# Recurrent attention and a two-layer feed-forward on one core: beta's halves exchanged by ScalarE, u's sign moved into a diagonal, GpSimd's low weight parts in one piece, and a new order of all steps

## The chip, the core and the metric

The kernel runs on one core of one Trainium2 chip. The metric is the device time of one execution in microseconds. The core's engines run side by side, each with its own queue in program order, and wait for each other by semaphores: TensorE (PE in the profile, PEld for its weight loads), VectorE (DVE), ScalarE (ACT), GpSimd (POOL) and SyncE (SP, which here only issues transfers).

## The reference

A recurrence over 768 time steps in 4 batches and 8 heads of width 48, and then a feed-forward over its 3072 rows of 384 numbers:

```python
for t in range(S):
    cur = np.einsum('bhd,bhe->bhde', u[None] * kt, vt)
    y[:, :, t] = np.einsum('bhd,bhde->bhe', rt, state + cur)
    state = wt[:, :, :, None] * state + np.einsum('bhd,bhe->bhde', kt, vt)
...
h = np.maximum(x @ w_in, 0.0)      # w_in is 384 x 2048
return (h * h @ w_out)             # w_out is 2048 x 384
```

The term with u gives each time step a number per head, the sum over d of r·u·k, which multiplies v of the same step. It is called beta below.

## The kernel before

The 768 steps are cut into 6 chunks of 128, and a unit is one chunk of one batch, 24 units in all (chunk c, batch b). Inside a unit the decays are multiplied up by scans on DVE (L538), r and k are scaled by them, TensorE makes a matrix of scores of 128 by 128 steps in quarters, and a mask keeps the part below the diagonal. The diagonal of that matrix is beta. ACT writes it as eight pieces of 64 columns, a constant diagonal times a column of beta each (L634, L749), before DVE lays the masked scores over it (L713, L763).

For chunk 0 beta comes from TensorE (L579). For the later chunks POOL multiplies r by k (L588) and by u (L590), and DVE sums over d (L593); `un` holds minus u in all rows, made so by one POOL instruction (L394), since k and the scores carry a minus sign. The sum has time steps in its 128 rows and the 8 heads in its columns, and the layout of the scores wants the lower 64 rows of one half of the heads exchanged with the upper 64 rows of the other half. Three DVE instructions of 64 rows by 4 columns do it, as the maximum of a number with itself (L596, L597, L598), the second and third each reading or overwriting what the one before has set free.

The feed-forward works in full precision by splitting each factor into a high part and a low part: three products instead of one. Both weight matrices come in 8 groups. For each group and matrix ("wi", "wo") ACT widens the raw bits (L430), DVE puts the number together in three instructions (L434, L438, L443), ACT rounds it to the high part (L450), and POOL subtracts to get the low part (L452), 768 columns in two instructions of 384. The plan marks DVE steps with `port=True` where it counts them as in POOL's way.

For one step f of the feed-forward (16 a chunk; the first six of chunk 0 and all of chunk 1 are cut into two halves of two batches) TensorE makes `hp` with nine products (L866), ACT takes the positive part (L871), ACT (chunk 0, L873) or DVE (later chunks, L875) squares it, ACT casts it to the high part of g (L877), DVE subtracts for the low part of g (L878), and TensorE adds three products a batch to `ob` (L884). PSUM holds two `hp`, two `a` and four `ob`.

The program is a list of steps, each with an engine, a cost and the keys that it reads and writes (`P.add`). The order in which they are issued is a table of step numbers (`ORDER`), found by a search outside the kernel; `PLACES` says which buffer a slot takes, and `FILLS` in front of which steps TensorE runs idle transposes (L352), and how many: `146: (3, 'hp', 0)` is three of them before step 146. Each engine's queue is this one order with the other engines' steps left out, SP's transfers too.

Of the kernel before, what the change touches and what calls it, by code (L numbers as in the profile page):

```python
# [9 lines left out]
F32 = mybir.dt.float32  # L10
# [4 lines left out]
AF = mybir.ActivationFunctionType  # L15
# [81 lines left out]
class Names:  # L97
# [133 lines left out]
def kernel(  # L231
# [50 lines left out]
    Q = C // 2  # L282
# [742 lines left out]
```

## Time and profile before

| | |
|---|---|
| median of 3 runs | 516.04 us (515.96 to 516.71) |
| the profiled execution | 517.37 us |
| its span, first to last instruction | 515.3 us, granted TensorE clock 0.997 |
| PE busy | 501.4 us, 97% of the span |
| PEld busy | 455.2 us, 88% |
| DVE busy | 359.6 us, 70% |
| ACT busy | 318.1 us, 62% |
| POOL busy | 107.0 us, 21% |
| idle transposes (L352) | 16 at the start, then 48 |

The shares are means over the whole span. The engines' load differs much between the first quarter and the rest, so they are read by stretches. A matrix product's end is modelled, and products overlap, so PE can be busy by this account and still lose a little.

### The profile page before, as it was taken

How to read it: one execution, taken by the hardware profiler on the slowest of the kernel's cores; microseconds unless marked ns; L12 is line 12 of the kernel's file. 1: busy time of each engine (PE TensorE's matmuls, PEld its weight loads, DVE VectorE, ACT ScalarE, POOL GpSimd, SP SyncE). 2: the span in 40 equal slices, each digit the busy share in tenths (PEclk: the TensorE clock that was granted, in tenths of full speed). 3: DMA queues.
4: the chain of work that ended last, by engine and by line, in shares of the span. 5: the costliest groups of instructions: out<-in, count | busy, mean ns of one | idle time of the engine just before them, and what ended most of it. 6: DMA issues, size and time to landing. Idle time of an engine off the chain costs nothing.

```text
span 515.3 us, 13724 instructions
## 1 busy us (share of the span) xinstructions
PE 501.4 (97%) x5416; PEld 455.2 (88%) x5416; DVE 359.6 (70%) x799; ACT 318.1 (62%) x870; POOL 107.0 (21%) x157
## 2 busy tenths in 40 slices
PE   8999999899999999999999999999999999999995
PEld 7888888789999999989998898898899888998894
DVE  6998899989778988868768477777466464324231
ACT  4999898889766767576564655663634353423232
POOL 2235951864040221303004002103000000000000
PEclk9999999999999999999999999999999999999998
DMA  8999899716837477483652662661161010200001
GB/s 161 222 225 251 184 207 194 138 21 93 153 56 123 90 107 141 80 137 55 103 115 54 118 99 33 103 123 37 39 115 32 1 21 12 67 1 1 1 0 66
DMA packets 188311, 48.73 MB, mean 95 GB/s; under 512 B 178001, under 2 KB 183122, under 8 KB 188242
## 3 DMA queue, kind: packets, MB, share of 16 engines
q1 hardware_dynamic: 187664, 47.01, 48.1%
q8 instruction: 44, 0.72, 0.6%
q10 hardware_dynamic: 578, 0.79, 0.4%
q14 instruction: 25, 0.20, 0.1%
HBM read 31.66 MB, written 4.72 MB: 71 GB/s over the span
## 4 chain that ended last, share of the span: by engine, by line
PE 81%; SPq 6%; DMA 4%; issue 3%; DVE 2%; ACT 2%; POOL 1%; POOLq 0%; DVEq 0%
PE ob L884 36%; PE hp L866 35%; PE ob L672 2%; SPq L507 2%; PE ob L691 2%; PE a L681 2%; SPq L474 2%; SPq L417 2%; PE a L654 1%; PE hp L639 1%; DMA st<-in_r_dram 1%; DMA ri<-in_moe_w_in_dram 1%; DMA v<-in_v_dram 1%; POOL wi L452 1%; ACT m L634 1%
## 5 line engine op out<-in xcount | busy, mean ns | idle before, releaser
L884 PE MATMUL ob<-wo,g 128*128 128x384 f32 x1152 | 226.7, 340 | 0.4 <-POOL wo L452 0.2
L866 PE MATMUL hp<-x,wi 128*128 128x512 f32 (+1 forms) x1062 | 222.2, 355 | 2.1 <-DVE g L878 1.4
L884 PEld LDWEIGHTS ob<-wo,g 128*128 128x128 f32 x1152 | 199.5, 188 | 8.7 <-DVE g L878 0.8
L866 PEld LDWEIGHTS hp<-x,wi 128*128 128x128 f32 x1062 | 174.9, 188 | 27.9 <-DVE g L878 2.4
L871 ACT ACTIVATE t<-hp 128x512 f32<-128x512 f32 (+1 forms) x118 | 61.0, 517 | 76.4 <-PE hp L866 48.6
L875 DVE SCALAR_TENSOR_TENSOR hp<-hp,t 128x512 f32<-128x512 f32 (+1 forms) x96 | 58.2, 606 | 69.6 <-ACT t L871 68.7
L878 DVE TENSOR_TENSOR g<-hp,g 128x512 fp32r<-128x512 f32 (+1 forms) x118 | 69.2, 587 | 38.5 <-ACT g L877 37.7
L877 ACT CAST g<-hp 128x512 fp32r<-128x512 f32 (+1 forms) x118 | 59.6, 506 | 46.1 <-DVE hp L875 45.2
L662 POOL MEMSET S<- 1x1 f32 x20 | 1.8, 88 | 242.4 <-PE ob L672 242.3
L634 ACT ACTIVATE m<-diag,beta 128x64 f32<-128x64 f32 x160 | 40.3, 340 | 1.2 <-DVE beta L597 1.1
L615 ACT ACTIVATE x<-ob 112x128 fp32r<-112x128 f32 x80 | 19.6, 278 | 22.6 <-PE ob L691 16.1
L618 DVE SCALAR_TENSOR_TENSOR x<-ob,x 112x128 fp32r<-112x128 f32 x80 | 20.8, 282 | 18.1 <-ACT x L615 15.7
L828 ACT COPY ob<-zero 112x128 f32<-112x128 f32 x80 | 20.6, 271 | 17.4 <-DVE x L618 10.9
L538 DVE TENSOR_TENSOR_SCAN pt<-pt,zero 112x128 f32<-112x128 f32 x64 | 25.8, 435 | 1.9 <-DMA v<-in_v_dram 1.1
L588 POOL TENSOR_TENSOR st<-st 128x384 f32<-128x384 f32 x20 | 22.0, 1107 | 22.4 <-DVE st L483 20.7
L452 POOL TENSOR_TENSOR wi<-q,wi 128x384 fp32r<-128x384 f32 x16 | 22.5, 1429 | 19.5 <-ACT wi L450 19.5
L452 POOL TENSOR_TENSOR wo<-q,wo 128x384 fp32r<-128x384 f32 x16 | 18.3, 1164 | 26.6 <-ACT wo L450 26.5
L590 POOL TENSOR_TENSOR st<-st,un 128x384 f32<-128x384 f32 x20 | 21.6, 1085 | 0.9
L483 DVE STREAM_TRANSPOSE st<-st 128x1152 f32<-128x1152 f32 x16 | 21.5, 1359 | 0.4 <-ACT st L609 0.4
L713 DVE COPY_PREDICATED m<-caus,a 128x256 f32<-128x256 uint8 x40 | 17.2, 441 | 3.2 <-PE a L654 3.1
L562 DVE TENSOR_TENSOR pt<-pt,m 112x512 f32<-112x512 f32 x24 | 18.0, 751 | 0.4
L545 ACT ACTIVATE m<-pt 112x512 f32<-112x512 f32 x24 | 15.2, 634 | 4.6 <-DVE pt L538 4.0
(126 smaller groups left out, 535.6 us busy)
## 6 DMA issues: line engine op xcount, KB each, us to landing
pt<-st SPq DMA_DIRECT2D x96, 96.0 KB, 3.0
ro<-in_moe_w_out_dram SPq DMA_DIRECT2D x8, 768.0 KB, 6.7
v<-in_v_dram SPq DMA_DIRECT2D x96, 48.0 KB, 2.9
out_dram<-q SPq DMA_DIRECT2D x20, 192.0 KB, 2.1
ri<-in_moe_w_in_dram SPq DMA_DIRECT2D x32, 96.0 KB, 5.2
ri<-in_moe_w_in_dram SPq DMA_DIRECT2D x8, 384.0 KB, 7.7
st<-in_k_dram SPq DMA_DIRECT2D x8, 384.0 KB, 5.2
st<-in_r_dram SPq DMA_DIRECT2D x8, 384.0 KB, 5.8
```

What stands on the lines that cost most here:

```text
L452: P.add("pool", 1.0, rank(8 * k + 5), lambda q=q, tt=tt, z=z: G.tensor_tensor(out=tt[:, 1, z * 384:z * 384 + 384], in0=q.tile[:, z * 384:z ...
L483: V.transpose(out=zt[:, i].rearrange("a t p q i -> a t (p q) i"), in_=sv[:, :, i].rearrange("s t p q x -> s t (p q) x"))
L538: lambda p=p: V.tensor_tensor_scan(out=pt[:, 0, p], data0=src(0)[:, p], data1=zero.broadcast_to([HP, C]), initial=1.0, op0=ALU.mult, op1=A ...
L588: P.add("pool", 0.97, rank("rk"), lambda: G.tensor_tensor(out=rk(), in0=rk(), in1=vals(2), op=ALU.mult), r=[(st, ui, 2)], w=[(st, ui, 1)])
L590: P.add("pool", 0.97, rank("ru"), lambda: G.tensor_tensor(out=rk(), in0=rk(), in1=un.rearrange("s (h d) -> s h d", d=D), op=ALU.mult), r=[ ...
L634: A.activation(M.tile[:, o:o + Q], diag2, AF.Copy, scale=beta.tile[:, i:i + 1])
L866: T.matmul(hp.tile[:, 0:n], wi[f][:, wl, kt], xT[:, kt, xl, xs], start=(m == 0), stop=(m == 3 * KT - 1))
L871: P.add("act", 0.49 if full else 0.28, rank("g1"), lambda: A.activation(t(), h(), AF.Relu), r=[hp], w=[(g, 1)])
L875: P.add("dve", 0.605 if full else 0.337, rank("g2"), lambda: V.scalar_tensor_tensor(out=h(), in0=h(), scalar=0.0, in1=t(), op0=ALU.max, op ...
L877: P.add("act", 0.48 if full else 0.26, rank("g3"), lambda: A.copy(out=hi(), in_=h()), r=[hp], w=[(g, 0)])
L878: P.add("dve", 0.605 if full else 0.335, rank("g4"), lambda: V.tensor_tensor(out=lo(), in0=h(), in1=hi().bitcast(F32), op=ALU.subtract), r ...
L884: T.matmul(obs[b][:, 0:DM], g.tile[0][:, gl, o:o + C], wo[f][:, wl], start=(f == 0 and m == 0), stop=(f == NF - 1 and m == 2))
```

## The change

Five things change.

1. Beta's exchange: three ACT copies take the place of the three DVE instructions. It is a step of ACT now, with 0.45 as cost in the plan.
2. u's sign: the POOL instruction on `un` goes. A second constant diagonal, `diag3`, the negative of the first, is made at the start by two scaled ACT copies, and the diagonals of chunks 1 to 5 are made from it.
3. POOL's low weight parts: one instruction of 768 columns for each group and matrix, 16 in place of 32. The keys ("rest", 0) and ("rest", 1) become one.
4. There are 17 steps fewer, so all numbers in the tables change.
5. The order, the places and the fills are those of a new search. The sum of the fills is 59 in place of 48.

```diff
 FILLS = {
-    15: (3, 'ob', 0), 56: (5, 'ob', 1), 58: (5, 'ob', 1), 37: (2, 'ob', 1), 42: (3, 'ob', 1), 83: (4, 'ob', 3), 146: (3, 'hp', 0), 125: (11, 'ob', 0),
-    128: (2, 'ob', 0), 130: (5, 'ob', 0), 166: (2, 'side', 0), 169: (3, 'side', 0),
+    14: (3, 'ob', 0), 30: (8, 'ob', 1), 55: (7, 'ob', 1), 71: (1, 'ob', 0), 48: (8, 'ob', 1), 82: (3, 'ob', 0), 89: (12, 'ob', 0), 145: (2, 'ob', 0),
+    463: (2, 'ob', 0), 159: (5, 'ob', 0), 127: (2, 'side', 0), 168: (6, 'side', 0),
 }
...
+    diag3 = at.tile([128, Q], F32, name="diag3")
...
         A.copy(out=diag2[hs], in_=ident[hs, hs])
+        A.activation(diag3[hs], ident[hs, hs], AF.Copy, scale=-1.0)
...
-        P.add("pool", 1.1, "un", lambda: G.tensor_scalar(out=un, in0=un, scalar1=-1.0, scalar2=None, op0=ALU.mult), w=["un"])
...
-            for z in range(2):
-                P.add("pool", 1.0, rank(8 * k + 5), lambda q=q, tt=tt, z=z: G.tensor_tensor(out=tt[:, 1, z * 384:z * 384 + 384], in0=q.tile[:, z * 384:z * 384 + 384], in1=tt[:, 0, z * 384:z * 384 + 384].bitcast(F32), op=ALU.subtract),
-                      r=[q, lead], w=[(nm, g, "rest", z)])
+            P.add("pool", 1.9, rank(8 * k + 5), lambda q=q, tt=tt: G.tensor_tensor(out=tt[:, 1], in0=q.tile, in1=tt[:, 0].bitcast(F32), op=ALU.subtract),
+                  r=[q, lead], w=[(nm, g, "rest")])
...
             def halves():
-                V.tensor_tensor(out=beta.tile[s1, H:], in0=beta.tile[s2, h1], in1=beta.tile[s2, h1], op=ALU.max)
-                V.tensor_tensor(out=beta.tile[s2, h1], in0=beta.tile[s1, h2], in1=beta.tile[s1, h2], op=ALU.max)
-                V.tensor_tensor(out=beta.tile[s1, h2], in0=beta.tile[s1, H:], in1=beta.tile[s1, H:], op=ALU.max)
-            P.add("dve", 0.46, rank("bh"), halves, w=[beta], port=True)
+                A.copy(out=beta.tile[s1, H:], in_=beta.tile[s2, h1])
+                A.copy(out=beta.tile[s2, h1], in_=beta.tile[s1, h2])
+                A.copy(out=beta.tile[s1, h2], in_=beta.tile[s1, H:])
+            P.add("act", 0.45, rank("bh"), halves, w=[beta])
...
-                            A.activation(M.tile[:, o:o + Q], diag2, AF.Copy, scale=beta.tile[:, i:i + 1])
+                            A.activation(M.tile[:, o:o + Q], diag2 if summed else diag3, AF.Copy, scale=beta.tile[:, i:i + 1])
```

What the new order makes of it is shown at three places. Line numbers of the changed kernel are smaller by one from L452 on (L878 becomes L877).

DVE near the end of chunk 0's feed-forward, before the change: the second reduction for beta, a low part of g, the first unit's exchange, and the next low part of g.

```order
L593 TENSOR_REDUCE beta_177<-st_143 128x8
L443 SCALAR_TENSOR_TENSOR q_156<-ro_70,q_156 128x768
L878 TENSOR_TENSOR g_95<-hp_151,g_95 128x256
L562 TENSOR_TENSOR pt_135<-pt_135,m_167 112x512
L596 TENSOR_TENSOR beta_176<-beta_176 64x4
L597 TENSOR_TENSOR beta_176<-beta_176 64x4
L598 TENSOR_TENSOR beta_176<-beta_176 64x4
L818 TENSOR_TENSOR S_140<-a_153,Ec_172 112x96
L878 TENSOR_TENSOR g_97<-hp_152,g_97 128x512
```

The same place on DVE after the change:

```order
L877 TENSOR_TENSOR g_99<-hp_152,g_99 128x256
L592 TENSOR_REDUCE beta_177<-st_144 128x8
L592 TENSOR_REDUCE beta_178<-st_144 128x8
L877 TENSOR_TENSOR g_95<-hp_153,g_95 128x512
L434 TENSOR_SCALAR q_156<-q_156 128x768
L438 SCALAR_TENSOR_TENSOR q_156<-ri_76,q_156 128x768
L555 TENSOR_TENSOR pt_136<-pt_136 112x4x127
L443 SCALAR_TENSOR_TENSOR q_156<-ri_76,q_156 128x768
L877 TENSOR_TENSOR g_97<-hp_152,g_97 128x512
```

Both reductions stand together ahead of a low part of g, the exchange is gone, and a weight's joining stands between two low parts of g.

ACT at the same place after the change: the positive part (L870), the square (L872) and the cast to the high part (L876) of a feed-forward step, and what stands between them and the next step's.

```order
L870 ACTIVATE t_98<-hp_152 128x512
L872 ACTIVATE hp_152<-t_98 128x512
L595 COPY beta_178<-beta_178 64x4
L596 COPY beta_178<-beta_178 64x4
L597 COPY beta_178<-beta_178 64x4
L876 CAST g_97<-hp_152 128x512
L430 ACTIVATE q_157<-ro_78 128x768
L827 COPY ob_151<-zero 112x128
L450 CAST wi_77<-q_156 128x768
L870 ACTIVATE t_100<-hp_153 128x512
L872 ACTIVATE hp_153<-t_100 128x512
L876 CAST g_99<-hp_153 128x512
```

The exchange of the first unit that gets one stands between the square and the cast of one step.

POOL's first weight parts, before the change:

```order
L394 TENSOR_SCALAR un<-un 128x384
L452 TENSOR_TENSOR wi_57<-q_155,wi_57 128x384 x2
L452 TENSOR_TENSOR wo_59<-q_156,wo_59 128x384 x2
L452 TENSOR_TENSOR wi_61<-q_155,wi_61 128x384 x2
L452 TENSOR_TENSOR wi_65<-q_156,wi_65 128x384 x2
```

And after it:

```order
L451 TENSOR_TENSOR wi_57<-q_156,wi_57 128x768
L451 TENSOR_TENSOR wo_59<-q_157,wo_59 128x768
L451 TENSOR_TENSOR wi_61<-q_156,wi_61 128x768
L451 TENSOR_TENSOR wi_65<-q_157,wi_65 128x768
L451 TENSOR_TENSOR wo_63<-q_156,wo_63 128x768
```

The negation is gone and each pair is one instruction; the sequence of these parts is the same.

## Rows read from the trace of the kernel before

**Rows 1.** Busy time by stretches: from:to, length, then each engine's busy us (instructions)

```profile
12.00:45.00 33.00, 30.77 (x485) 27.14 (x484) 31.44 (x66) 31.17 (x93) 12.42 (x9) 1.00 0.99 226
45.00:130.00 85.00, 81.44 (x833) 72.81 (x837) 78.84 (x144) 76.98 (x190) 48.11 (x43) 1.00 0.74 148
130.00:430.00 300.00, 299.73 (x3579) 273.98 (x3569) 214.73 (x512) 176.87 (x523) 43.37 (x83) 1.00 0.47 83
```

**Rows 2.** PE's waits in the whole span: us in total, times, longest

```profile
PE a L352 <- POOL ident masks.py:199: 1.6, 1, 1.6
PE hp L866 <- DVE g L878: 1.4, 2, 0.8
PE ob L691 <- issue: 1.3, 2, 1.2
...
PE hp L866 <- POOL wi L452: 0.6, 1, 0.6
PE hp L639 <- DVE g L878: 0.4, 1, 0.4
...
PE hp L521 <- DVE g L878: 0.3, 1, 0.3
PE ob L884 <- POOL wo L452: 0.2, 1, 0.2
```

**Rows 3.** Timeline of PE at 41 and 77 us: start, us, what, idle before

```profile
41.50 2.18 PE L866 MATMUL hp<-x,wi 128*128 128x256 f32 x16 [0.55 <-POOL wi L452]
...
77.07 1.67 PE L866 MATMUL hp<-x,wi 128*128 128x512 f32 x6 [0.79 <-DVE g L878]
```

**Rows 4.** Timeline of DVE from 72.5 us: start, us, what

```profile
72.55 0.41 DVE L878 TENSOR_TENSOR g<-hp,g 128x256 fp32r<-128x256 f32 x1
...
74.06 1.02 DVE L596 TENSOR_TENSOR beta<-beta 64x4 f32<-64x4 f32 x1
75.12 0.95 DVE L597 TENSOR_TENSOR beta<-beta 64x4 f32<-64x4 f32 x1
76.10 0.15 DVE L598 TENSOR_TENSOR beta<-beta 64x4 f32<-64x4 f32 x1
...
76.35 0.67 DVE L878 TENSOR_TENSOR g<-hp,g 128x512 fp32r<-128x512 f32 x1
```

**Rows 5.** Timeline of POOL, two stretches: start, us for both halves, idle before

```profile
37.41 4.03 POOL L452 TENSOR_TENSOR wi<-q,wi 128x384 fp32r<-128x384 f32 x2 [4.08 <-ACT wi L450]
...
70.79 2.71 POOL L452 TENSOR_TENSOR wi<-q,wi 128x384 fp32r<-128x384 f32 x2 [3.49 <-ACT wi L450]
74.05 2.00 POOL L452 TENSOR_TENSOR wo<-q,wo 128x384 fp32r<-128x384 f32 x2 [0.55 <-ACT wo L450]
```

**Rows 6.** Groups of instructions from 0 to 130 us: count, busy us, mean ns

```profile
L597 DVE TENSOR_TENSOR beta<-beta 64x4 f32<-64x4 f32 x6 | 3.0, 494 | 0.2
L596 DVE TENSOR_TENSOR beta<-beta 64x4 f32<-64x4 f32 x6 | 2.4, 402 | 0.1
```

**Rows 7.** Timeline of DVE from 123 us: start, us, what

```profile
123.18 1.39 DVE L597 TENSOR_TENSOR beta<-beta 64x4 f32<-64x4 f32 x1
...
127.60 0.42 DVE L878 TENSOR_TENSOR g<-hp,g 128x256 fp32r<-128x256 f32 x1
```

**Rows 8.** Timeline of ACT at 127 us: start, us, what

```profile
127.21 0.36 ACT L877 CAST g<-hp 128x256 fp32r<-128x256 f32 x1
```

**Rows 9.** Groups of instructions in the whole span: count, busy us, mean ns

```profile
L561 ACT COPY Ec<-pt 112x4 f32<-112x4 f32 x20 | 3.9, 195 | 1.5 <-DVE pt L538 1.5
L452 POOL TENSOR_TENSOR wi<-q,wi 128x384 fp32r<-128x384 f32 x16 | 22.5, 1429 | 19.5 <-ACT wi L450 19.5
```

**Rows 10.** Timeline of ACT at the start: start, us, what, idle before

```profile
2.10 0.50 ACT L365 COPY diag<-ident 64x64 f32<-64x64 f32 x2
...
6.17 0.69 ACT L548 ACTIVATE pt<-ob,one_sided 112x512 f32<-112x512 f32 x1 [3.57 <-PE ob L521]
```

**Rows 11.** Timeline of PE at 27 us: start, us, what

```profile
27.12 1.42 PE L352 MATMUL ob<-ident 128*128 128x128 f32 x11
```

More of the change, by code (lines that the diff above doesn't have):

```diff
@@ L859, in ffn @@
         hp, g = Slot("hp"), Slot("g")
-        wkeys = lambda nm: [(nm, f // 2, "lead"), (nm, f // 2, "rest", 0), (nm, f // 2, "rest", 1)]
+        wkeys = lambda nm: [(nm, f // 2, "lead"), (nm, f // 2, "rest")]
         def first():
```

203 rows, old and new, of tables (ORDER, PLACES) are left out of this document.

## The prediction, made before the run

> **What bounds the kernel now.** I read the busy time by stretches first [rows 1]. From 130 to 430 us TensorE (PE) is busy 299.73 of 300 us. No other engine is near that: VectorE (DVE) has 214.73 us and ScalarE (ACT) 176.87 us in the same stretch. What a change saves on those two after 130 us is saved off the path. Between 12 and 130 us it is otherwise. PE is idle for 5.8 us there (33 - 30.77 and 85 - 81.44), and DVE and ACT are both above 90%, above 94% between 12 and 45 us. In this stretch the weights are split, and chunk 0's feed-forward runs beside the attention of chunks 0 and 1. The time that can still be won or lost lies there.
>
> Second I read what PE waited for [rows 2]. The ten rows of that view add up to 7.1 us; 1.6 us of it is the start. The largest cause is DVE's low part of g (1.4 + 0.4 + 0.3), then GpSimd's (POOL) low weight parts (0.6 + 0.2). A cause without an engine, "issue", has 1.3 us.
>
> Third I went to the places in the order of time. At 77.07 us a first matrix product starts after 0.79 us of idle time, released by a DVE g, and at 41.50 us one after 0.55 us, released by POOL's low part of wi [rows 3]. Ahead of the g for the first, DVE ran beta's three exchange instructions without a gap [rows 4]. They move four numbers a row. The third took 0.15 us; the first took 1.02 and the second 0.95 us. POOL shows why: its two half parts of wo run from 74.05 to 76.05 us, 1.0 us each [rows 5], and the first and second exchange end when the first and second half end. A DVE instruction that reads two operands from SBUF stood still until POOL's was over. The same happens in the other direction: two half parts of wi took 4.03 us from 37.41 us on [rows 5].
>
> **The change, part by part.** The sums are against the profiled execution's own 517.37 us (span 515.3, 2.07 around it). The median of the runs is 516.04, 1.33 lower, and each difference is taken off the median as it stands.
>
> *The exchange leaves DVE.* Sixty instructions go. By the first paragraph only the six trios before 130 us can matter. Their first two instructions were busy 3.0 + 2.4 us [rows 6], the third 0.15 us each: 6.3 us, where unblocked ones would take 2.7. What of it reached PE I read at two places. The trio from 74.06 us took 2.1 us and stands ahead of the g that PE waited 0.79 us for: that wait goes, -0.8 us. In the trio from 122.38 us the second instruction alone took 1.39 us; DVE has no gap from there to the g at 127.60 us [rows 7], for which PE waited 0.4 us [rows 2]. But ACT's cast, which that g needs, ended at 127.57 us [rows 8], so two causes ended together; I take half, -0.2 us. Together -1.0 us. Bounds: nothing, if the new order puts other DVE work there, and -2.1 us, all of PE's waits on DVE's g.
>
> *ACT takes it.* No row shows this copy on ACT; the nearest is the copy of four columns, 195 ns [rows 9]. The three depend on each other, so I take no overlap: 0.59 us a trio, 3.5 us for the six before 130 us. ACT has 8.0 us of idle time between 45 and 130 us (85 - 76.98), which can hide most. But the order above shows the first trio between the square and the cast of one feed-forward step: the cast, DVE's g and PE's second product queue behind it. I take +0.6 us for this one place and nothing for the other five. Bounds: 0 and +3.5 us. The fourteen trios after 130 us, 8.2 us, lie under PE's work. The copies also wait for DVE's reduction, with ACT's later instructions behind that wait; at the place shown the reduction stands ahead of the g before, so I take nothing.
>
> *POOL's parts whole.* Sixteen instructions of 768 columns in place of 32 of 384. Two halves without interference take 2.00 us [rows 5], so I take 2.0 for a whole; a half of wi took 1.43 us in the mean [rows 9], a pair 2.9. A pair can be held up by DVE twice, a whole once. The pair of 4.03 us would become 2.0 plus one DVE instruction of about 1 us (the 1.02 of rows 4 is the longest hold there), 1.0 us earlier, and the 0.55 us of PE's wait at 41.50 go, with the 0.2 for wo: -0.8 us. Bounds: 0 and -0.8; what speaks for a loss is the second rival.
>
> *u's negation.* One POOL instruction less before POOL's first weight part, which itself waits for ACT; nothing. Against it two scaled copies on ACT at the start, like the two of 0.50 us at 2.10 us; the instruction after these waits 3.57 us for PE [rows 10], which hides them (+0.5 us if it didn't). The diagonal's instructions stay as many and as long.
>
> *Fillers.* The table lets PE run 59 filler transposes and not 48 (the sixteen at the start apart). Eleven took 1.42 us [rows 11]. They stand where the table expects PE to be idle, and 5.8 us of idle time are there: nothing; +1.4 us if they stand in the way.
>
> *The order.* Every engine's order is new; the number of matrix products and the last rows of PE and ACT are as before, so the 12 to 130 us stretch is what can differ. I can price it only from both sides: it can win the 3.7 us of PE's waits that are left (7.1 less the start's 1.6 and the 1.8 above), and it can as well make as many new ones. I take 0.
>
> Sum: -1.0 + 0.6 - 0.8 = -1.2 us. 517.37 becomes 516.17 for a profiled execution like this one, and 516.04 becomes **514.8 us**.
>
> Here a rule of the Trainium skill is weighed. The row first: an exchange instruction lasted 1.02 us where its like takes 0.15, beside a POOL half part of 1.0 us [rows 4, 5]. The page "SBUF — State Buffer", section "Who interferes with whom", says that DVE and GpSimd share a pair of ports, that it is an exclusive lock, and that a DVE instruction with two SBUF inputs and a GpSimd instruction that reads SBUF block each other for a whole instruction. The trace agrees. Worked on, the rule speaks against the whole parts: one lock would last about 2.0 us and not 1.0.
>
> **The rivals.**
> (a) *Nothing measurable, 516.0 us.* ACT is nearly as full as DVE before 130 us, so the work only changes hands: three trios in the way in place of one are +1.8 us, against the 1.0 and 0.8 gained. For it speaks ACT's load, against it ACT's 8.0 us of idle time. It decides if three of the six trios stand directly ahead of a cast that PE waits for.
> (b) *Slower, 517.8 us: DVE stands behind whole parts.* Today a DVE instruction with two SBUF inputs that meets a half part loses up to 1.0 us, then runs before the second half. Behind a whole it loses up to 2.0 us. Three of the sixteen pieces meeting DVE like this ahead of a g, 1.0 us more each, cost PE 3.0 us, less the 1.2 gained. It passes no change when two such meetings reach PE. Against it: POOL holds the ports for as long in total as before, and a DVE instruction that reads PSUM ran at its usual 0.41 us at 72.55 us [rows 4] while POOL's parts from 70.79 us on took 2.71 us [rows 5]. This is the page's rule as this kernel would feel it; no run here shows a whole part yet.
> (c) *Slower, 517.4 us: fillers and order.* If the eleven fillers come where PE has work (+1.4), the sum is +0.2; one more wait of PE like the 1.2 us that is the longest of "issue" makes 517.4. For it: more fillers mean that the table itself expects more idle time.
> (d) *Much faster, 512.7 us*, if the new order also removes 2.1 of the 3.7 us that I left. Nothing in the rows shows that it does.
> That the exchange stays on DVE in some form is excluded by the order's rows.
>
> **How the numbers follow.** 0.2% of 516 us, 1.03 us, is about what a measurement of this kernel can tell from no change. The forecast has 0.38; (d) 0.05; (a) 0.28; (b) 0.16; (c) 0.13. Faster is the forecast and (d), 0.43; the same is (a), 0.28; slower (b) and (c), 0.29. The time is the forecast's 514.8. Cases of both signs share the chance, so the forecast's own range stands beside: 513.7 (DVE's bound of -2.1 in place of -1.0) to 515.0. The whole range, 512.8 to 517.8, takes in (a), (c) and (b) at its price and leaves out (d) and the order's full loss of 3.7 us.
>
> **What would show it.** Right: no wait of PE over 0.5 us on DVE's g between 70 and 130 us, none on POOL's parts, POOL's 16 instructions at 2.0 to 3.0 us, ACT's trios at about 0.6 us, PE idle for less than 4.6 us between 12 and 130 us. Wrong: DVE instructions of 0.15 to 0.95 us that last 2 us beside a POOL part (b); casts of g on ACT late behind trios (a); PE's waits moved to another releaser, or fillers with no wait after them (c). What I can least defend is the zero for the order.

## The result: 0.7% slower, and the profile after

The changed kernel takes 520.88 us (median of 7 runs, 519.5 to 521.06), the kernel before 516.61 us beside it on the same chip (515.35 to 518.13). The ratio is 1.0073 with a 95% interval of 1.0053 to 1.0093, so 3.8 us are lost where 1.2 were to be won. Prices below are ratios times 516.6 us, because each experiment has its own runs of before beside it. The profiled execution took 519.85 us, its span is 518.1 us at a granted clock of 0.997. One single run below, of 529.37 us and of the kernel without fillers, lay over 1.5% above the fastest of its kernel and is left out of the ratio as slow.

First the busy time by stretches, which answers to [rows 1].

```profile
12.00:45.00 33.00, 32.47 (x500) 28.55 (x499) 30.93 (x67) 31.04 (x90) 7.59 (x4) 1.00 1.05 222
45.00:130.00 85.00, 79.14 (x798) 69.72 (x797) 73.73 (x118) 74.13 (x186) 43.28 (x31) 1.00 0.69 147
130.00:430.00 300.00, 299.52 (x3588) 273.56 (x3587) 209.33 (x471) 187.37 (x581) 43.52 (x83) 1.00 0.48 84
```

From 130 to 430 us PE is as full as before. From 12 to 45 us it is idle for 0.53 us and not 2.23; the fillers' own time there grew only from 4.8 to 5.3 us, so most of that is products. From 45 to 130 us it is idle for 5.86 us and not 3.56, and in this stretch DVE, ACT and POOL are all busy for less time than before: none is overloaded, they come too late. How late is read from the starts of DVE's low parts of g. The ninth, the eleventh and the eighteenth of them, first in the kernel before:

```profile
63.37 0.41 DVE L878 TENSOR_TENSOR g<-hp,g 128x256 fp32r<-128x256 f32 x1
...
69.03 0.42 DVE L878 TENSOR_TENSOR g<-hp,g 128x256 fp32r<-128x256 f32 x1
...
104.37 0.69 DVE L878 TENSOR_TENSOR g<-hp,g 128x512 fp32r<-128x512 f32 x1 [0.63 <-ACT g L877]
```

In the changed kernel the ninth starts here, and the other two at 70.27 and 108.96 us, in the timeline further down:

```profile
62.57 0.42 DVE L877 TENSOR_TENSOR g<-hp,g 128x256 fp32r<-128x256 f32 x1 [0.49 <-ACT g L876]
```

The ninth is 0.8 us early, the eleventh 1.2 us late and the eighteenth 4.6; the last of all is 3.2 us late. So the loss arises between 63 and 110 us. The waits of PE answer to [rows 2]:

```profile
PE hp L865 <- DVE g L877: 2.6, 4, 1.5
PE ob L883 <- DVE g L877: 2.2, 1, 2.2
...
PE ob L883 <- ACT ob L827: 0.7, 2, 0.4
```

The waits on POOL's parts are gone, as forecast, and so is the one on "issue". In their place g costs PE 5.3 us (with 0.5 of a third row) and not 2.1, and two waits are most of it. The timelines of PE, DVE, POOL and ACT around them:

```profile
70.73 0.50 PE L865 MATMUL hp<-x,wi 128*128 128x512 f32 x1 [1.52 <-DVE g L877]
...
109.69 0.44 PE L883 MATMUL ob<-wo,g 128*128 128x384 f32 x1 [2.16 <-DVE g L877]
...
67.29 1.37 DVE L434 TENSOR_SCALAR q<-q 128x768 uint32<-128x768 uint32 x1
68.58 1.76 DVE L443 SCALAR_TENSOR_TENSOR q<-ri,q 128x768 uint32<-128x768 uint32 x1
70.27 0.41 DVE L877 TENSOR_TENSOR g<-hp,g 128x256 fp32r<-128x256 f32 x1
...
105.02 2.33 DVE L562 SCALAR_TENSOR_TENSOR m<-pt,m 112x512 f32<-112x512 f32 x1
...
108.96 0.67 DVE L877 TENSOR_TENSOR g<-hp,g 128x512 fp32r<-128x512 f32 x1
...
66.63 2.90 POOL L589 TENSOR_TENSOR st<-st,un 128x384 f32<-128x384 f32 x2
...
104.72 2.08 POOL L451 TENSOR_TENSOR wo<-q,wo 128x768 fp32r<-128x768 f32 x1 [0.64 <-ACT wo L450]
...
67.41 0.37 ACT L876 CAST g<-hp 128x256 fp32r<-128x256 f32 x1
...
105.68 0.56 ACT L876 CAST g<-hp 128x512 fp32r<-128x512 f32 x1
```

At both places ACT's cast was done long before DVE subtracted: at 67.78 us, with g at 70.27, and at 106.24, with g at 108.96. DVE had other work queued ahead of g, and that work took longer beside POOL's. At 67 us a weight step (one of the three DVE instructions that put a weight together) of 0.55 us took 1.37 and the next, usually 0.95, took 1.76 beside two products with u. At 105 us a key step (one of those that make the scaled k) of 0.68 us took 2.33 beside a whole weight part.

Three groups of the changed kernel, over the whole span and, for the copy, from 0 to 130 us:

```profile
L451 POOL TENSOR_TENSOR wi<-q,wi 128x768 fp32r<-128x768 f32 x8 | 16.3, 2040 | 48.6 <-ACT wi L450 43.6 <-DMA v<-in_v_dram 4.9
L352 PE MATMUL ob<-ident 128*128 128x128 f32 x59 | 8.8, 279 | 0.0
...
L595 ACT COPY beta<-beta 64x4 f32<-64x4 f32 x4 | 0.8, 192 | 0.1
```

A whole part of wi takes 2.04 us in the mean (one of wo 1.87), a copy on ACT 0.19, as estimated. Only four trios stand before 130 us now, where six stood.

### The profile page after: what moved, and what is told of

Its sections match the earlier page's. It is cut to its first block, busy times and chain, and to the rows that moved or that the text cites. A ratio compares the mean times of both kernels' runs of the same rounds, so it can differ in the third digit from the quotient of the medians.

```text
span 518.1 us, 13730 instructions
## 1 busy us (share of the span) xinstructions
PE 503.4 (97%) x5427; PEld 455.3 (88%) x5427; DVE 351.1 (68%) x739; ACT 328.2 (63%) x932; POOL 97.5 (19%) x140
## 4 chain that ended last, share of the span: by engine, by line
PE 73%; DVE 2%; ACT 2%; DMA 1%; issue 0%; SPq 0%; POOL 0%; ACTq 0%; POOLq 0%
PE ob L883 33%; PE hp L865 32%; PE ob L671 2%; PE ob L690 2%; PE a L680 2%; PE a L653 1%; PE hp L638 1%; DMA v<-in_v_dram 1%; DVE st L482 0%; DVE g L877 0%; DVE pt L555 0%; ACT x L614 0%; DVE m L562 0%; ACT g L876 0%; DVE x L617 0%
## 5 line engine op out<-in xcount | busy, mean ns | idle before, releaser
L870 ACT ACTIVATE t<-hp 128x512 f32<-128x512 f32 (+1 forms) x118 | 61.0, 517 | 72.0 <-PE hp L865 44.7
L877 DVE TENSOR_TENSOR g<-hp,g 128x512 fp32r<-128x512 f32 (+1 forms) x118 | 69.2, 587 | 47.7 <-ACT g L876 47.0
L876 ACT CAST g<-hp 128x512 fp32r<-128x512 f32 (+1 forms) x118 | 59.4, 504 | 43.2 <-DVE hp L874 42.4
L451 POOL TENSOR_TENSOR wi<-q,wi 128x768 fp32r<-128x768 f32 x8 | 16.3, 2040 | 48.6 <-ACT wi L450 43.6
L589 POOL TENSOR_TENSOR st<-st,un 128x384 f32<-128x384 f32 x20 | 23.6, 1183 | 0.9
L451 POOL TENSOR_TENSOR wo<-q,wo 128x768 fp32r<-128x768 f32 x8 | 15.0, 1873 | 22.3 <-ACT wo L450 19.6
L562 DVE SCALAR_TENSOR_TENSOR m<-pt,m 112x512 f32<-112x512 f32 x24 | 18.8, 782 | 0.4
L555 DVE TENSOR_TENSOR pt<-pt 112x508 f32<-112x508 f32 x24 | 18.9, 790 | 0.1
L561 DVE TENSOR_TENSOR pt<-pt,m 112x512 f32<-112x512 f32 x24 | 16.8, 699 | 2.9 <-ACT m L545 2.3
```

The lines of the kernel that those rows point to most:

```text
L451: P.add("pool", 1.9, rank(8 * k + 5), lambda q=q, tt=tt: G.tensor_tensor(out=tt[:, 1], in0=q.tile, in1=tt[:, 0].bitcast(F32), op=ALU.subtr ...
L589: P.add("pool", 0.97, rank("ru"), lambda: G.tensor_tensor(out=rk(), in0=rk(), in1=un.rearrange("s (h d) -> s h d", d=D), op=ALU.mult), r=[ ...
L870: P.add("act", 0.49 if full else 0.28, rank("g1"), lambda: A.activation(t(), h(), AF.Relu), r=[hp], w=[(g, 1)])
L876: P.add("act", 0.48 if full else 0.26, rank("g3"), lambda: A.copy(out=hi(), in_=h()), r=[hp], w=[(g, 0)])
L877: P.add("dve", 0.605 if full else 0.335, rank("g4"), lambda: V.tensor_tensor(out=lo(), in0=h(), in1=hi().bitcast(F32), op=ALU.subtract), r ...
```

## The experiments

The theories: **L**, whole parts hold DVE longer than halves; **A**, ACT is the limit and the copies cost its chain; **O**, the new order puts DVE's work ahead of a g that PE needs; **C**, fillers stand in the way; later **H**, the holds by POOL (a DVE instruction lasts longer because POOL is at work) make DVE late at the two places.

**The edits in the old order.** Three kernels keep the order and fillers of before: `e1_old_act` with the exchange alone, `e1_old_whole` with the whole parts alone, `e1_old_all` with these and the negative diagonal.

```diff
 # e1_old_act, e1_old_all
-                V.tensor_tensor(out=beta.tile[s1, H:], in0=beta.tile[s2, h1], in1=beta.tile[s2, h1], op=ALU.max)
+                A.copy(out=beta.tile[s1, H:], in_=beta.tile[s2, h1])
...
 # e1_old_whole, e1_old_all: the later half's step is empty
-... lambda q=q, tt=tt, z=z: G.tensor_tensor(out=tt[:, 1, z * 384:z * 384 + 384], ...
+... lambda q=q, tt=tt, z=z: z or G.tensor_tensor(out=tt[:, 1], in0=q.tile, ...
```

> The order before with beta's exchange on ACT, and nothing else changed. Theory A: slower than before by 0.6 to 2 us. Theories L and O: 0 to 1 us faster, and PE's wait of 0.79 us at 77 us is gone.

> The order before with GpSimd's parts whole, and nothing else changed. Theory L: slower than before by 1 to 3 us (ratio 1.002 to 1.006), with DVE instructions of 2 us beside parts. Theory O: within 0.8 us of before. Theory A: as before.

> The order and the fillers of the kernel before, with the three edits: ACT copies, GpSimd's parts whole, the negative diagonal. Theory L (whole parts hold DVE for 2 us ahead of a low part of g): slower than before by 0.5 to 2 us, since the edit carries its fault into any order. Theory O (the new order and its fillers lose the time, and the edits are harmless): 0 to 1.2 us faster than before, ratio 0.998 to 1.000. Theory A (ACT's copies stand ahead of casts): slower by 0.6 to 2 us, as in the run with the copies alone.

Measured: copies alone 1.0077 (1.0053 to 1.0101), whole parts alone 1.0050 (1.0024 to 1.0077), all three 1.0066 (1.0044 to 1.0089). So in the old order each edit loses by itself, 4.0 and 2.6 us, and they don't add. With all three the old order is as slow as the new one with them (1.0073): kept with these edits, the order makes no difference that can be told. PE's waits on g are 4.6 us in the profile of all three, 2.1 before and 5.3 in the changed kernel. For the copies the timelines of DVE, POOL, ACT and PE show where:

```profile
114.90 1.93 DVE L434 TENSOR_SCALAR q<-q 128x768 uint32<-128x768 uint32 x1
...
128.96 0.42 DVE L878 TENSOR_TENSOR g<-hp,g 128x256 fp32r<-128x256 f32 x1 [0.83 <-ACT g L877]
...
114.44 1.98 POOL L588 TENSOR_TENSOR st<-st 128x384 f32<-128x384 f32 x2
...
123.72 0.19 ACT L596 COPY beta<-beta 64x4 f32<-64x4 f32 x1
123.94 0.19 ACT L597 COPY beta<-beta 64x4 f32<-64x4 f32 x1
124.16 0.19 ACT L598 COPY beta<-beta 64x4 f32<-64x4 f32 x1
...
76.73 1.43 PE L866 MATMUL hp<-x,wi 128*128 128x512 f32 x5 [0.26 <-DVE g L878]
...
119.07 1.20 PE L866 MATMUL hp<-x,wi 128*128 128x512 f32 x4 [0.79 <-DVE g L878]
```

At 77 us the wait of 0.79 us [rows 3] is 0.26: two thirds of what was forecast. At 119 us a new one of 0.79 us arises. The same place in the kernel before:

```profile
114.81 0.85 DVE L434 TENSOR_SCALAR q<-q 128x768 uint32<-128x768 uint32 x1
...
114.12 2.41 POOL L588 TENSOR_TENSOR st<-st 128x384 f32<-128x384 f32 x2
```

ACT, and POOL behind it, run 0.3 us later with the copies, so that POOL's two products of r and k begin at 114.44 us and not at 114.12; the weight step that DVE starts at nearly the same time as before (114.90, then 114.81) lasts 1.93 us where it had taken 0.85, and a g stands behind it. Before, the step was over 0.5 us after the first product ended, and the second took 1.43 us instead of 1.0; now both products take 1.0 and the step ends 0.4 us after the second. That is not the time of a copy but a changed meeting of DVE and POOL. The copies' own cost comes next: from 121.6 us on ACT runs without a gap, a trio stands in it, and DVE, which had no gap there [rows 7], waits 0.83 us for the cast. This g is 1.4 us later than before, the one at 121.56 us only 0.7: about the 0.57 us of one trio, so theory A has a part in the loss. The profiled run (518.50 us) was the fastest of six, and its span is 1.4 us longer than that of before, so it locates a third of the loss; where the rest lies is open.

For the whole parts, DVE and POOL, and PE's waits on g:

```profile
62.00 2.48 DVE L443 SCALAR_TENSOR_TENSOR q<-ro,q 128x768 uint32<-128x768 uint32 x1
...
72.19 0.55 DVE L593 TENSOR_REDUCE beta<-st 128x8 f32<-128x384 f32 x1
72.65 2.15 DVE L443 SCALAR_TENSOR_TENSOR q<-ro,q 128x768 uint32<-128x768 uint32 x1
...
61.02 2.64 POOL L452 TENSOR_TENSOR wi<-q,wi 128x768 fp32r<-128x768 f32 x1
...
71.80 2.18 POOL L452 TENSOR_TENSOR wi<-q,wi 128x768 fp32r<-128x768 f32 x1 [4.53 <-ACT wi L450]
...
PE hp L866 <- DVE g L878: 1.8, 3, 1.0
...
PE ob L884 <- DVE g L878: 0.6, 1, 0.6
```

The same two weight steps beside halves, in the kernel before:

```profile
61.80 1.65 DVE L443 SCALAR_TENSOR_TENSOR q<-ro,q 128x768 uint32<-128x768 uint32 x1
...
71.29 1.34 DVE L443 SCALAR_TENSOR_TENSOR q<-ro,q 128x768 uint32<-128x768 uint32 x1
```

Each stands directly ahead of a g and is 0.8 us longer beside a whole part. PE waits 0.98 us for the first of these g's (before: 0.64) and 0.64 us for the second (before: nothing). So this is L, and it accounts for 1.0 us of PE's time; the run's loss of 2.6 us is not all located, since the span of its profile is only 0.8 us longer than before.

**The edits taken back in the new order.** `e1_new_half` issues each low part in two halves again, `e2_new_dve` puts the exchange back on DVE, `e2_new_half_dve` does both.

```diff
 # e1_new_half, e2_new_half_dve
-... lambda q=q, tt=tt: G.tensor_tensor(out=tt[:, 1], ...
+... lambda q=q, tt=tt: [G.tensor_tensor(out=tt[:, 1, z * 384:z * 384 + 384], ...) for z in range(2)],
 # e2_new_dve, e2_new_half_dve: the three DVE lines of before in place of A.copy
```

> The changed kernel with GpSimd's low parts in two halves again, the order and the fillers new. Theory L: 2 to 3 us faster than the changed kernel (ratio to before 1.002 to 1.004), and PE's wait of 2.16 us at 109 us falls to 1.2 us or less. Theory O: within 0.7 us of the changed kernel (ratio 1.006 to 1.009). Theory A: as O.

> The changed kernel with beta's exchange back on DVE, at the places where the new order has ACT's copies. Theory A (the copies cost ACT's chain): 1 to 3 us faster than the changed kernel, ratio 1.001 to 1.005. Theory O: 0 to 1.5 us slower than the changed kernel, ratio 1.007 to 1.010, since DVE is the late engine in the new order.

> The new order and fillers with the exchange on DVE and the low parts in halves: of the edits only the negative diagonal is left. Theory O: as slow as the changed kernel or slower, ratio 1.006 to 1.011. Theories A and L (the edits cost, the order doesn't): within 1 us of before.

Measured: halves 1.0072 (1.0050 to 1.0095), the same as the changed kernel, so L is not the cause there. DVE and POOL of that run at the second place:

```profile
105.40 1.51 DVE L562 SCALAR_TENSOR_TENSOR m<-pt,m 112x512 f32<-112x512 f32 x1
...
107.29 1.04 DVE L565 TENSOR_TENSOR pt<-pt,m 112x512 f32<-112x512 f32 x1
...
105.10 2.69 POOL L451 TENSOR_TENSOR wo<-q,wo 128x384 fp32r<-128x384 f32 x2 [0.64 <-ACT wo L450]
```

One hold of 1.65 us became two, of 0.83 and 0.36, on two instructions that both stand ahead of the same g; PE still waited 1.81 us for that g, and not 2.16. At the first place, where POOL's products with u and no weight part are in the way, it waited 1.81 us and not 1.52, so nothing is left of the gain. With the exchange on DVE the ratio is 1.0193 (1.0173 to 1.0213), with both taken back 1.0166 (1.0144 to 1.0188). In the new order ACT's copies are worth some 6 us, so A is refuted for it. With the exchange on DVE, PE's waits on g are 6.8 us where the changed kernel has 5.3, and a new one on DVE stands behind them:

```profile
PE ob L883 <- DVE x L617: 1.8, 1, 1.8
```

Without the copies and the whole parts, the new order (with its buffers, its fillers and the negative diagonal) is 8.6 us worse than the old. It is no better than the old one even for the code it was found for.

**The fillers.** `e2_new_nofill` has `FILLS = {}`.

> The changed kernel without its 59 fillers (the sixteen at the start stay). Theory C (fillers stand in the way of PE's work): 1 to 3 us faster than the changed kernel, ratio 1.001 to 1.005. Theory O: within 1 us of the changed kernel, since the late engine is DVE; where PE stood idle instead, the granted clock may fall and the kernel be slower.

Measured: 1.0109 (1.0085 to 1.0133), some 1.9 us slower than the changed kernel, though the two intervals just overlap. The granted clock of its stretch from 12 to 45 us, third number from the end, is 0.87 where it was 1.00, with PE idle for 3 us there:

```profile
12.00:45.00 33.00, 29.98 (x416) 26.10 (x415) 28.56 (x60) 27.95 (x84) 5.75 (x3) 0.87 1.03 216
```

C is refuted: taking the fillers out wins nothing.

**Two low parts of g moved ahead.** `e2_new_moved` puts four numbers behind others in the table. 537 and 596 are the two late low parts of g; 379 and 393 are weight steps, 272 and 273 key steps, all on DVE. `e3_place1` and `e3_place2` make one move each.

```diff
 # e3_place1, e2_new_moved
-392, 379, 393, 534, 535, 536, 199, 200, 531, 424, 537, 540,
+392, 534, 535, 536, 199, 200, 531, 424, 537, 379, 393, 540,
 # e3_place2, e2_new_moved: 272 and 273 go from before 443 and 436 to here
-596, 600,
+596, 272, 273, 600,
```

> The changed kernel with one low part of g put ahead of two weight steps on DVE (the g that ended PE's wait of 1.52 us at 70.73 us) and another put ahead of two key steps (the one that ended the wait of 2.16 us at 109.69). Everything else as changed. Theory O (the new order puts DVE work ahead of a g that PE needs): both waits fall below 0.5 us and the kernel is 2 to 3.5 us faster than the changed one, ratio to before 1.000 to 1.004. Theory A (ACT is the limit, so the time comes back at the next wait for ACT): less than 1 us faster, ratio 1.005 to 1.008.

> The changed kernel with only the first of the two moves: at 70 us the low part of g ahead of two weight steps on DVE. Theory O (each wait is a price of its own): 1.5 us faster than the changed kernel, ratio 1.003 to 1.006. Rival A (whoever is late there, the 109 us place takes the time back): as the changed kernel, ratio about 1.008.

> The changed kernel with only the second of the two moves: at 109 us the low part of g ahead of two key steps on DVE. Theory O: 1.5 to 2.5 us faster than the changed kernel, ratio 1.002 to 1.006, and the two single moves add up to the 4 us of both. Rival A: less than 1 us faster.

Measured: both 0.9996 (0.9981 to 1.0011), 4.0 us faster than the changed kernel and level with before. The first alone 1.0061 (1.0042 to 1.0081), the second alone 1.0023 (1.0008 to 1.0038): 0.6 and 2.6 us. The 0.6 us is less than the 1.5 forecast and not clear of the noise, so the gain is shown for both moves together and for the second. No other engine's sequence differs. PE's longest waits on ACT and on g that are left, and DVE at 68 us:

```profile
PE ob L883 <- ACT ob L827: 1.6, 2, 1.2
PE hp L865 <- DVE g L877: 1.4, 3, 0.7
...
67.82 0.42 DVE L877 TENSOR_TENSOR g<-hp,g 128x256 fp32r<-128x256 f32 x1 [0.51 <-ACT g L876]
68.16 1.43 DVE L434 TENSOR_SCALAR q<-q 128x768 uint32<-128x768 uint32 x1
```

The weight step is held as long as ever (1.43 us), but behind g PE does not wait for it. A new wait of 1.2 us for ACT has come up at 107 us.

**The holds taken away, the order kept.** `e4_new_nohold` leaves out POOL's products with u for two units, and at one weight POOL writes zeros in place of the low part.

```diff
+... G.memset(tt[:, 1].bitcast(F32), 0.0) if (g, k) == (6, 1) else G.tensor_tensor(out=tt[:, 1], ...
-        P.add("pool", 0.97, rank("ru"), lambda: G.tensor_tensor(
+        P.add("pool", 0.97, rank("ru"), lambda: c == 1 and b < 2 or G.tensor_tensor(
```

> The changed kernel in its own order, with GpSimd's work taken away where it held DVE ahead of the two late g's: the products with u of chunk 1's first two units are left out (about 66.6 to 69.5 us), and the low part of one group of w_out (104.7 us) is a memset of zero, so beta lacks u there and that group's low part is missing. Theory H (the hold makes DVE late there): both waits fall below 0.7 us without any move, 2 to 4 us faster than the changed kernel, ratio 1.000 to 1.004. Theory O alone (the order makes it late, whatever GpSimd does): less than 1.2 us faster, ratio 1.005 to 1.008.

Measured: 0.9963 (0.9945 to 0.9982), 5.7 us faster than the changed kernel. DVE at both places, and PE's waits:

```profile
66.93 0.55 DVE L434 TENSOR_SCALAR q<-q 128x768 uint32<-128x768 uint32 x1
67.40 0.95 DVE L443 SCALAR_TENSOR_TENSOR q<-ri,q 128x768 uint32<-128x768 uint32 x1
...
101.95 0.67 DVE L562 SCALAR_TENSOR_TENSOR m<-pt,m 112x512 f32<-112x512 f32 x1
...
PE hp L865 <- DVE g L877: 1.0, 3, 0.5
...
PE ob L883 <- DVE g L877: 0.6, 1, 0.6
```

The steps have their own durations again, the first wait is gone and the second is 0.6 us, in an order that was not touched. H holds, and O alone falls: it takes DVE work ahead of g and a hold on that work. The gain is more than the 2 to 4 us expected: the waits on g fell by 3.7 us (5.3 to 1.6), and where the other 2.0 us come from is open. The run does less work, so its time is no version's time.

**Can more be had in this way?** `e3_moved2` adds three moves to the two, at 59, 79 and 105 us; `e3_moved2_half` is that with halves; `e4_new_moved3` adds only those at 59 and 105 us, the latter smaller; `e5_new_moved4` is that with the g at 110 us moved as well; `e4_old_moved` moves two g's in the kernel before. All are edits of the table like the ones above, for example

```diff
 # e4_old_moved: 409 is a weight step, 540 a low part of g; 210 the exchange, 568 a low part of g
-408, 409, ... 540, ... 210, ... 568,
+408, ... 540, 409, ... 568, 210,
```

> Both moves and three more: at 59 us the cast and the low part of g ahead of two scalings on ACT and a weight step on DVE; at 79 us the cast ahead of the exchange and the low part of g ahead of a weight step; at 105 us the two key steps behind the small x steps too. Theory O: PE's waits of 0.7, 0.4 and 1.2 us at these places go, 1 to 2.3 us faster than with two moves, ratio to before 0.995 to 0.998. Rival A (ACT is the limit there, work moved behind a cast only comes back): no faster than before, ratio 0.998 to 1.002.

> The kernel with all five moves, and GpSimd's low parts in halves again. Theory L (a whole part holds DVE longer than a half): 0.5 to 2 us faster than with whole parts. Theory O (with the g's ahead, what DVE loses behind POOL is hidden either way): within 0.7 us of it.

> The changed kernel with the two moves, that at 59 us, and at 105 us only one small x step put ahead of the two key steps; the exchange at 79 us stays ahead of its cast. Theory O: 1 to 1.8 us faster than with two moves, ratio to before 0.996 to 0.998. Rival A: as with two moves, ratio 0.999 to 1.001.

> The kernel of the run before (moves at 59, 70, 105 and 109 us), and the next low part of g, which PE waited 1.25 us for at 110 us, ahead of one weight step, two state steps and a mask on DVE. Theory O: that wait falls below 0.4 us, 0.9 to 1.3 us faster than that kernel, ratio to before 0.996 to 0.9985. Rival A (the time comes back at the next wait): ratio 0.999 to 1.001.

> The kernel before with two low parts of g put ahead of DVE work: the one that PE waited 0.64 us for at 63.84 us ahead of a weight step, and the one of 0.79 us at 77.07 us ahead of the exchange. Theory O: both waits go, 0.8 to 1.4 us faster than before, ratio 0.997 to 0.9985. Rival A: the time comes back at the next wait, ratio 0.999 to 1.002.

Measured: 1.0000 (0.9982 to 1.0017), 1.0021 (1.0005 to 1.0036), 0.9997 (0.9980 to 1.0014), 1.0001 (0.9982 to 1.0019) and 1.0016 (0.9995 to 1.0038). None beats the kernel before, and halves with five moves are no faster than whole parts, so L falls here too. In the four others rival A was right that the time comes back, though not always at ACT: it came back at another step of DVE or ACT. In `e3_moved2` and `e4_new_moved3` PE waits 1.3 us for a later g, at 110 us. In `e4_old_moved` the weight step that stood ahead of the g now stands ahead of a scan that reads `hp` from PSUM (a wait of 0.94 us at 66.5 us), and the next unit's exchange, whose first two instructions took 0.16 us each before, now meets two POOL halves ahead of another such scan and takes 1.02 and 0.94 us (a wait of 1.50 us at 85.7 us). In `e5_new_moved4` PE waits for ACT's zeroing of `ob`. One row of PE's waits from each of these two runs:

```profile
PE hp L866 <- DVE pt L538: 2.4, 2, 1.5
```

```profile
PE ob L883 <- ACT ob L827: 2.4, 3, 1.4
```

**The copies after 130 us.** `e4_old_act_late` is `e1_old_act` with chunk 1 left on DVE.

```diff
+            swap = (lambda o, i: A.copy(out=o, in_=i)) if c > 1 else (lambda o, i: V.tensor_tensor(out=o, in0=i, in1=i, op=ALU.max))
```

> The order before, with the exchange on ACT for chunks 2 to 5 only; chunk 1's four units, whose trios lie before 130 us, keep DVE's. The prediction's step (trios after 130 us lie under PE's work): as before, ratio 0.998 to 1.002. Rival: 1 to 2 us slower, ratio 1.002 to 1.004, the half of the copies' loss that the profiled run did not show.

Measured: 1.0014 (0.9995 to 1.0033). Whether the late copies cost up to 1.7 us or nothing can't be told from this; if the two parts add, some 3 of the copies' 4.0 us lie before 130 us.

## Why the prediction was wrong, step by step

**What bounds the kernel.** Right: the loss arises before 130 us, and PE's waits on DVE's g are the part of it that can be named. They grew by 3.2 us, while PE's other waits fell by 1.7. The span as a whole grew by 2.8 us, of which PE's idle time is 0.8 (14.7 us and not 13.9) and its busy time 2.0 (503.4 and not 501.4). Fillers count as busy and take 1.0 us more (12.5 and not 11.5, the sixteen at the start among them); the other 1.0 us is products, and why they took longer is open.

**The exchange leaves DVE, -1.0 us; ACT takes it, +0.6.** In the old order the wait at 77 us fell by 0.5 of the 0.8 us that were forecast [rows 3, 4]. The rest was mis-sized. In the old order the copies cost 4.0 us on balance. Located of it are a trio in an ACT chain without gaps, which [rows 8] had shown the end of, and a hold of DVE that became 1.1 us longer when ACT and POOL ran 0.3 us later. In the new order, moving the exchange to ACT is worth some 6 us, with PE's waits on DVE the ones that grow when it is moved back. A saving or a cost of 3 us in DVE or ACT time can't be priced apart from the order it stands in.

**POOL's parts whole, -0.8 us.** PE's waits on POOL's parts did go, but the pieces' length changed nothing in the new order (1.0072 against 1.0073), and in the old it cost 2.6 us. The second rival's mechanism, a hold of 2 us ahead of a g, is shown in both kernels: 2.33 us for a step of 0.68 in the new order, and 2.48 and 2.15 us in the old for steps of 0.95 that took 1.65 and 1.34 beside halves. Against it the prediction had put that POOL's total time stays; the new order bears that out in part, since cutting the parts took only 0.35 us off the wait at 109 us.

**Fillers, 0.** No loss from them is seen; without them it is some 1.9 us more. That half of the third rival was wrong.

**The order, 0.** This is the step that failed, and with it the sum. At two places the new table puts DVE steps that POOL can hold ahead of a low part of g that ACT had long made ready. Putting the two g's ahead gives 4.0 us back, taking the holds away 5.7. The bound of 3.7 us for the order's loss was near the 4.0 us, the likeliest value of 0 was not. Even with the bound the sum gives 2.5 us lost and not 3.8, because the 1.2 us of savings is missing too: with the two g's ahead the kernel is level with before (0.9996, 0.2 us), and no further move brought it lower. Nor is the order a price by itself. It loses 8.6 us without the copies and the whole parts, and next to nothing against the old order that has them (1.0073 and 1.0066). The prediction could have come nearer: the front's second piece of the new order, a neighbour of the two places, shows weight steps between two g's, and [rows 4] shows what a DVE step can become beside POOL. It asked which waits the edits remove, and not which DVE steps that POOL can hold the new order puts ahead of which g, and what POOL does at that time.

**u's negation, 0.** Not tried alone.

The Trainium skill's page "SBUF — State Buffer", section "Who interferes with whom", says that a `tensor_scalar` can take both ports and be blocked too, and that `tensor_reduce` on trn2 never contends. The traces agree with both: 1.37 us for L434's 0.55 at 67.29 us of the changed kernel, and an undisturbed 0.55 us for L593 at 72.19 us of `e1_old_whole`, in the middle of a whole part.

## What to carry to other kernels

Where a new order is searched together with edits, read the order first: list for each result that the bound engine waits for what stands ahead of it on its engine's queue, and whether another engine can stretch that. An edit's price belongs to its order; the same copies cost 4 us in one and earned 6 in the other. A wait that is moved away pays only if the steps behind it have slack: two moves won 4.0 us, and two or three more won nothing.

## What was not expected of the hardware

A shift of 0.3 us between DVE and POOL made a DVE step of 0.85 us one of 1.93. In both runs the step began while POOL's first product ran; in one it was over soon after that product, in the other only after the second. What decides between the two the traces don't show, but small edits far away change it. Splitting a POOL instruction of 2.08 us into two halves freed DVE little sooner, because the second half met another DVE instruction: 2.33 us for one became 1.51 and 1.04 for two, where 0.67 each is usual, and the g behind them was waited for 0.35 us less. And 59 idle transposes of 8.8 us on the engine that bounds the kernel are no loss: without them the granted clock was 0.87 from 12 to 45 us, where it was 1.00 with them, and the kernel some 1.9 us slower.
